# Attention over a cached K and V with a squared-ReLU gate: PV turned to queries on partitions, and FFN, projections and out-projection as fillers

## The chip, the core and the metric

The kernel runs on one core of one Trainium2 chip. The metric is device time in microseconds (us) of one execution, the median of three runs. Before the change it is 1469.16 us (1469.04 to 1469.86).

The engines are named as the profile names them: PE multiplies matrices (PEld is its weight load), DVE and ACT work on vectors, POOL on small things, and SP issues DMAs. SBUF holds tiles of 128 partitions, PSUM holds the results of PE in banks of 512 f32 columns per partition.

## The reference

x has 2048 rows of 512. There are 32 heads of width 128, each with 2048 cached keys and values. All inputs are bf16.

```
xn = (x - mean) / sqrt(var + 1e-5)
q  = xn @ wq                        # 32 heads of 128
p  = softmax(q @ k_cache^T * 128**-0.5)
s  = (p @ v_cache) @ wo             # [2048, 512]
h  = relu(xn @ w1 + b1) ** 2        # [2048, 1792]
g  = silu(h @ w2 + b2)
out = x + s * g
```

## The kernel before, in words

Queries are cut into 4 blocks of 512 (index j), keys into 16 tiles of 128, taken in 8 pairs. One pair of key tiles of one head of one block is a step (index `pi`, 4 x 32 x 8 = 1024 of them); a head of a block has the index `g` (128 of them), the step within it is `k`.

The program is written as one list of instructions per engine, in the order in which the Python code emits them; each engine runs its list strictly in that order, and waits on semaphores where an operand or a buffer needs it. So the place of a call in the code decides what queues behind what.

It has two stages. The first one, which the code calls phase A, loads the whole of x transposed (`xnT`, features on partitions), does the layernorm in that form with ones-matmuls for the sums, and then the FFN of all four blocks (`gen_ffn`: 14 chunks of 128 hidden features, `gen_hT`, `gen_relu_sq`, `gen_o2`), up to the gate `g_all` of all 2048 queries. Its SBUF is then given free, and everything of the second stage that may reuse it waits for the end of phase A.

The second stage runs the 1024 steps (L805). A step emits two score matmuls into `psA` (`gen_scores`, keys on partitions, 512 queries on columns, two buffers of 1024 columns), an exp on ACT into `pT` (`gen_exp`), additions of `pT` into `accD` on DVE for the denominators (`gen_den_adds`), extras, and the PV of two steps earlier (`gen_pv`). PV has V as weights and 512 columns of `pT` moving; its result in `psB` has head features on partitions and queries on columns.

Since the queries lie on columns, a denominator per query has to be spread over all 128 partitions. `gen_headend_A` (in step k = 2 of the next head) sums `accD` over partitions by four 1-column matmuls, takes the reciprocal, and writes it onto the diagonals of `diag_t`; `gen_headend_B` (k = 4) multiplies ones by `diag_t` into `psC`, copies it to `rrep`, and multiplies `psB` by it into `oT_all`. The other extras are the projection of the head after next (`gen_proj`, 4 matmuls into `psC` and a copy to `qt_sb`) and, from block 1 on, one out-projection matmul of the block before in four of the eight steps (`gen_post_tasks`, 32 heads accumulated in `psD` for one tile of 128 queries, then times `g_all` plus x). The last block's out-projection stands behind the loop.

K is loaded by a transposing DMA on SP's queue two heads ahead into three buffers, V and `wq` by plain ones.

All matmuls go through one helper (L149), so the profile tells them apart by their tiles.

Of the kernel before, what the change touches and what calls it, by code (L numbers as in the profile page):

```python
# [43 lines left out]
class _Sched:  # L44
# [42 lines left out]
    def emit(self, eng, fn, deps=()):  # L87
        waits = self._resolve(eng, deps)
        idx = eng.n
        eng.n += 1  # L90
        eng.prog.append((waits, fn, ("cnt",)))
        return _Tok(eng.sem, idx + 1, dict(eng.known))
# [58 lines left out]

def _act(e, out, in_, func, scale=1.0, bias=0.0):
    return e.activation(out, in_, func, bias=bias, scale=scale)  # L153
# [28 lines left out]
def _iota(e, out):  # L182
    return e.iota(out, [[1, out.shape[-1]]], base=0, channel_multiplier=-1,
                  allow_small_or_imprecise_dtypes=True)
# [15 lines left out]
def bass_recurrent_scan__mha_block_cached__dense_activation_squared_relu__prompt_kernel(  # L200
# [12 lines left out]
    dbg_xnT=None,  # L213
    dbg_g=None,
    dbg_s=None,
    stage="full",
# [4 lines left out]
    assert Dh == P and D % P == 0 and D <= 512 and F % P == 0  # L221
    assert Sq % 512 == 0 and Sk % (2 * P) == 0
    QB = 512
    NQT = Sq // P
# [9 lines left out]
    NPAIR = NG * NPR  # L234

# [8 lines left out]
    ones = nc.alloc_sbuf_tensor("ones", [P, P], BF16)  # L244
    ident = nc.alloc_sbuf_tensor("ident", [P, P], BF16)
    xnT = nc.alloc_sbuf_tensor("xnT", [P, NDC, Sq], BF16)
    g_all = nc.alloc_sbuf_tensor("g_all", [P, NQT, D], BF16)

    psA = nc.alloc_psum_tensor("psA", [P, 4 * 512], F32)
    psB = nc.alloc_psum_tensor("psB", [P, 2 * 512], F32)  # L250
    psC = nc.alloc_psum_tensor("psC", [P, 512], F32)
    psD = nc.alloc_psum_tensor("psD", [P, 512], F32)

    def bankA(i):
        return psA[:, i * 512:(i + 1) * 512]

    def bankB(i):
        return psB[:, i * 512:(i + 1) * 512]

    sl_out = [S.slot("out0"), S.slot("out1")]  # L260
    sl_dbg = S.slot("dbg")

    from contextlib import ExitStack
    stackA = ExitStack()
    sbA = lambda shape, dt, name: stackA.enter_context(nc.sbuf_tensor(name, shape, dt))
    xT_sq = sbA([P, NQB, NDC, QB], BF16, "xT_sq")
    var_t = sbA([P, NQB, QB], F32, "var_t")
    lnv_t = sbA([P, NQB, QB], F32, "lnv_t")
    rstd_t = sbA([P, NQB, QB], BF16, "rstd_t")
    w1_sb = sbA([P, NDC, F], BF16, "w1_sb")  # L270
    w2_sb = sbA([P, NFC, D], BF16, "w2_sb")
    r_t = sbA([P, 2, QB], BF16, "r_t")
    NH2 = 3
    h2T = sbA([P, NH2, QB], BF16, "h2T")
    sig_t = sbA([P, 2, D], BF16, "sig_t")
    identf = sbA([P, P], F32, "identf")
    b1b = sbA([P, NFC], BF16, "b1b")
    b1f = sbA([P, NFC], F32, "b1f")
    b2row = sbA([P, D], BF16, "b2row")
    _phaseA_hwm = nc.sbuf_base  # L280

    t_ones = E(GP, partial(_memset, out=ones[:], val=1.0))
    t_idf = E(GP, partial(_iota, out=identf[:]))
    t_ident = E(GP, partial(_ts, out=ident[:], in0=identf[:], scalar1=0.0, scalar2=None,
                           op0=ALU.is_equal), deps=[t_idf])

    sl_x = [S.slot(f"xT{c}") for c in range(NDC)]
    sl_w = S.slot("wmisc")

    tok_xc = [None] * NDC  # L290
    for c in range(NDC):
        tok_xc[c] = S.emit_dma(
            SP, partial(_dmaT, out=xnT[:, c, :], in_=A_x[0, :, c * P:(c + 1) * P]),
            sl_x[c])
    tok_x = tok_xc[-1]
    S.emit_dma(SP, partial(_dma, out=w1_sb[:], in_=B_w1.rearrange("(c p) f -> p c f", p=P)),
               sl_w, group_done=False)
    S.emit_dma(SP, partial(_dma, out=w2_sb[:], in_=B_w2.rearrange("(c p) d -> p c d", p=P)),
               sl_w, group_done=False)
    S.emit_dma(SP, partial(_dma_gather, nc, out=b1b[:], in_=B_b1.rearrange("(c p) -> p c", p=P)),  # L300
               sl_w, group_done=False)
    tok_w = S.emit_dma(SP, partial(_dma, out=b2row[0:1, :],
                                   in_=B_b2.rearrange("(o d) -> o d", o=1)),
                       sl_w, group_done=True)
    t_b1 = E(DV, partial(_copy, out=b1f[:], in_=b1b[:]), deps=[tok_w])

    invD = 1.0 / float(D)
    assert NQB <= 4, "LN schedule assumes <= 4 query blocks (psA banks)"
    t_scale_last = [None] * NQB
    t_psA_reader = [None] * 4  # L310
    t_sums = [None] * NQB
    for j in range(NQB):
        js = slice(j * QB, (j + 1) * QB)
        for c in range(NDC):
            t_sums[j] = E(PE, partial(_mm, out=bankA(j)[:, :], lhsT=ones[:, :], rhs=xnT[:, c, js],
                                      start=(c == 0), stop=(c == NDC - 1)),
                          deps=[t_ones, tok_xc[c]])
    t_ctr_all, t_sq_all = [], []
    for j in range(NQB):
        js = slice(j * QB, (j + 1) * QB)  # L320
        t_ctr = []
        for c in range(NDC):
            t_ctr.append(E(DV, partial(_stt, out=xnT[:, c, js], in0=bankA(j)[:, :], scalar=-invD,
                                       in1=xnT[:, c, js], op0=ALU.mult, op1=ALU.add),
                           deps=[t_sums[j]]))
        t_psA_reader[j] = t_ctr[-1]
        t_ctr_all.append(t_ctr)
        t_sq = []
        for c in range(NDC):
            t_sq.append(E(AC, partial(_act, out=xT_sq[:, j, c, :], in_=xnT[:, c, js],  # L330
                                      func=ACT.Square),
                          deps=[t_ctr[c]]))
        t_sq_all.append(t_sq)
    t_ss_reader = [None, None]
    t_v = [None] * NQB
    for j0 in range(0, NQB, 2):
        grp = list(range(j0, min(j0 + 2, NQB)))
        t_ss = {}
        for j in grp:
            s = j % 2  # L340
            psS = psC if s == 0 else psD
            for c in range(NDC):
                t_ss[j] = E(PE, partial(_mm, out=psS[:, :], lhsT=ones[:, :], rhs=xT_sq[:, j, c, :],
                                       start=(c == 0), stop=(c == NDC - 1)),
                            deps=[t_sq_all[j][c], t_ss_reader[s], t_ones])
        for j in grp:
            s = j % 2
            psS = psC if s == 0 else psD
            t_v[j] = E(DV, partial(_ts, out=var_t[:, j, :], in0=psS[:, :], scalar1=invD,
                                   scalar2=LN_EPS, op0=ALU.mult, op1=ALU.add),  # L350
                       deps=[t_ss[j]])
            t_ss_reader[s] = t_v[j]
    t_l = [None] * NQB
    for j in range(NQB):
        t_l[j] = E(AC, partial(_act, out=lnv_t[:, j, :], in_=var_t[:, j, :], func=ACT.Ln),
                   deps=[t_v[j]])
    t_r = [None] * NQB
    for j in range(NQB):
        t_r[j] = E(AC, partial(_act, out=rstd_t[:, j, :], in_=lnv_t[:, j, :], func=ACT.Exp,
                               scale=-0.5),  # L360
                   deps=[t_l[j]])
    for j in range(NQB):
        js = slice(j * QB, (j + 1) * QB)
        t_sc = None
        for c in range(NDC):
            t_sc = E(DV, partial(_tt, out=xnT[:, c, js], in0=xnT[:, c, js],
                                 in1=rstd_t[:, j, :], op=ALU.mult),
                     deps=[t_r[j], t_sq_all[j][c]])
        t_scale_last[j] = t_sc

    t_g_done = [None] * NQT
    t_gtile_reader = [None] * TPB
    t_psB_reader = [None, None]
    t_r_reader = [None, None]
    t_h2_reader = [None] * NH2
    t_sig_reader = [None, None]
    ffn_state = {"chunk_ctr": 0}

    def gen_ffn(j):
        js = slice(j * QB, (j + 1) * QB)  # L380

        def gen_bias():
            for qt in range(TPB):
                E(PE, partial(_mm, out=bankA(qt)[:, 0:D], lhsT=ones[0:1, 0:P], rhs=b2row[0:1, 0:D],
                              start=True, stop=False),
                  deps=[tok_w, t_ones, t_gtile_reader[qt], t_psA_reader[qt]])

        def gen_hT(c, slot_b):
            t = None
            for dc in range(NDC):  # L390
                t = E(PE, partial(_mm, out=bankB(slot_b)[:, :],
                                  lhsT=w1_sb[:, dc, c * P:(c + 1) * P], rhs=xnT[:, dc, js],
                                  start=(dc == 0), stop=(dc == NDC - 1)),
# [28 lines left out]
        for c in range(NFC):  # L422
# [3 lines left out]
            if c == min(1, NFC - 1):  # L426
                gen_bias()
# [438 lines left out]
```

## Time and profile before

| what | value |
|---|---|
| median of 3 runs | 1469.16 us (1469.04 to 1469.86) |
| profiled execution, span | 1469.5 us |
| PE / DVE / ACT busy | 1305.6 / 1171.9 / 1055.7 us |
| phase A (layernorm, FFN) | from 0 to about 163 us |
| attention steps | from about 163 to 1429 us |
| out-projection of the last block, output | from about 1429 us on |
| mean granted TensorE clock | 0.983 |

The page gives each engine's busy time with its share of the span, the chain of work that ended last, and groups of instructions (line, engine, operation, tile written <- tiles read, shape, count, busy us, mean ns of one, idle time just before and what ended it). A row of a stretch (windows) has the engines' busy times in turn, with counts in brackets, the granted clock, the share in which the 16 DMA engines were busy, and GB/s. A timeline row has start, length, engine, instruction. Matmuls overlap in a stream, so the mean time of one is longer than the distance from one start to the next.

### The profile page before, as it was taken

To read this page: it belongs to the slowest core of one execution; us is meant where nothing else is said; L and a number is where in the kernel's file an instruction comes from. 1 tells how busy PE (TensorE), PEld (TensorE's weight loads), DVE (VectorE), ACT (ScalarE), POOL (GpSimd) and SP (SyncE) were. 2 spreads that over 40 slices of the span, in tenths; PEclk is the share of its full clock that TensorE was granted. 3 is DMA by queue.
4 is the path that set the end of the run, shared out by engine and by line. 5 is a ranking of instruction groups with operands and counts; after the bars stand their busy time and mean duration, and the time that the engine had idled before them with its cause. 6 is when DMAs were issued, how large, how long until landed. Compare 5 with 4: busy or idle time off the path is not lost.

```text
span 1469.5 us, 17842 instructions
## 1 busy us (share of the span) xinstructions
PE 1305.6 (89%) x6640; PEld 572.3 (39%) x6640; DVE 1171.9 (80%) x2117; ACT 1055.7 (72%) x1069; POOL 19.7 (1%) x43
## 2 busy tenths in 40 slices
PE   3899888888888999999999999999999999999987
PEld 0334333333333444444444444444444444444433
DVE  2666688888888888888888888888888888888871
ACT  2210588887778888888888888888888888888860
POOL 0000000000000000000000000000000000000001
PEclk7899999999999999999999999999999999999999
DMA  9100267777666656655755665655655665666510
GB/s 227 31 0 0 41 128 158 157 151 149 119 124 129 124 110 128 128 119 115 136 112 122 129 121 113 136 114 116 134 118 120 125 130 110 130 125 121 113 36 25
DMA packets 616265, 166.33 MB, mean 113 GB/s; under 512 B 608754, under 2 KB 614643, under 8 KB 616179
## 3 DMA queue, kind: packets, MB, share of 16 engines
q1 hardware_dynamic: 614642, 160.99, 55.3%
q0 software_dynamic: 1536, 4.20, 0.8%
q8 instruction: 53, 0.87, 0.3%
q14 instruction: 34, 0.27, 0.1%
HBM read 93.85 MB, written 2.10 MB: 65 GB/s over the span
## 4 chain that ended last, share of the span: by engine, by line
PE 60%; DVE 23%; ACT 13%; issue 2%; SPq 1%; DMA 1%; DVEq 0%; POOL 0%
PE psA L149 22%; PE psB L149 22%; ACT pT L153 12%; PE psC L149 11%; DVE accD L157 10%; DVE diag_t L157 6%; PE psD L149 6%; DVE rden_b L171 2%; DVE rden_t L175 1%; DVE tmp_t L157 1%; SPq L192 1%; ACT xT_sq L153 1%; DVE out_t L157 1%; DVE g_all L157 1%; DMA b2row<-in_B_b_dram 1%
## 5 line engine op out<-in xcount | busy, mean ns | idle before, releaser
L153 ACT ACTIVATE pT<-psA 128x1024 bf16<-128x1024 f32 x1024 | 1026.0, 1024 | 237.2 <-PE psA L149 214.6
L157 DVE TENSOR_TENSOR accD<-accD,pT 128x1024 bf16<-128x1024 bf16 x896 | 617.9, 690 | 173.9 <-ACT pT L153 149.2
L149 PE MATMUL psA<-qt_sb,kT 128*128 128x512 bf16 x2048 | 610.2, 380 | 0.3 <-ACT pT L153 0.3
L149 PE MATMUL psB<-pT,v_sb 128*128 128x512 bf16 x2048 | 609.0, 379 | 0.3 <-ACT pT L153 0.3
L149 PEld LDWEIGHTS psA<-qt_sb,kT 128*128 128x128 bf16 x2048 | 196.8, 98 | 247.2 <-ACT pT L153 26.2
L149 PEld LDWEIGHTS psB<-pT,v_sb 128*128 128x128 bf16 x2048 | 185.4, 98 | 182.8 <-ACT pT L153 1.1
L149 PE MATMUL psD<-wo_all,oT_all 128*128 128x512 bf16 x512 | 176.4, 385 | 2.4 <-DVE tmp_t L157 2.4
L149 PE MATMUL psC<-xnT,wq_sb 128*128 128x512 bf16 x512 | 152.7, 381 | 3.4 <-DVE qt_sb L171 3.2
L149 PE MATMUL psC<-diag_t,ones 128*128 128x128 bf16 x512 | 51.0, 222 | 113.0 <-DVE diag_t L157 113.0
L149 PEld LDWEIGHTS psC<-diag_t,ones 128*128 128x128 bf16 x512 | 29.0, 98 | 175.5 <-DVE diag_t L157 175.5
L157 DVE TENSOR_TENSOR diag_t<-ident,rden_b 128x512 bf16<-128x512 bf16 x128 | 88.6, 692 | 4.4
L157 DVE TENSOR_TENSOR oT_all<-psB,rrep 128x512 bf16<-128x512 f32 x128 | 88.5, 691 | 4.4
L171 DVE CAST qt_sb<-psC 128x512 bf16<-128x512 f32 x128 | 87.5, 683 | 2.0 <-PE psC L149 2.0
L171 DVE CAST rrep<-psC 128x512 bf16<-128x512 f32 x128 | 87.5, 684 | 0.7 <-PE psC L149 0.7
L153 ACT ACTIVATE sig_t<-psA 128x512 bf16<-128x512 f32 x16 | 9.1, 596 | 105.4 <-PE psA L149 104.3
L149 PEld LDWEIGHTS psD<-wo_all,oT_all 128*128 128x128 bf16 x512 | 50.4, 99 | 65.3 <-DVE tmp_t L157 3.8
L149 PEld LDWEIGHTS psC<-xnT,wq_sb 128*128 128x128 bf16 x512 | 47.7, 97 | 71.0 <-issue 38.3
L163 DVE TENSOR_SCALAR r_t<-psB,b1f 128x512 bf16<-128x512 f32 x56 | 42.0, 750 | 27.9 <-PE psB L149 27.9
L149 PE MATMUL psB<-xnT,w_sb 128*128 128x512 bf16 x224 | 59.4, 392 | 4.9 <-DVE xnT L157 4.9
L149 PE MATMUL psA<-w_sb,h2T 128*128 128x512 bf16 x224 | 58.5, 384 | 4.5 <-DVE h2T L157 4.5
L157 DVE TENSOR_TENSOR accD<-accD 128x512 bf16<-128x512 bf16 x128 | 54.4, 425 | 4.4
L171 DVE COPY accD<-pT 128x1024 bf16<-128x1024 bf16 x128 | 53.3, 417 | 1.2 <-ACT pT L153 1.2
(37 smaller groups left out, 289.0 us busy)
## 6 DMA issues: line engine op xcount, KB each, us to landing
v_sb<-in_A_v_cache_dram SPq DMA_DIRECT2D x128, 512.0 KB, 4.7
wq_sb<-in_A_wq_dram SPq DMA_DIRECT2D x128, 128.0 KB, 4.7
wo_all<-in_A_wo_dram SPq DMA_DIRECT2D x4, 1024.0 KB, 6.1
w_sb<-in_B_w_dram SPq DMA_DIRECT2D x2, 1792.0 KB
kT<-in_A_k_cache_dram SPq DMA_TRANSPOSE x128, 4.6
x_t<-in_A_x_dram POOLq DMA_DIRECT2D x16, 128.0 KB, 3.9
out_dram<-out_t POOLq DMA_DIRECT2D x16, 128.0 KB, 3.7
xnT<-in_A_x_dram SPq DMA_TRANSPOSE x4, 5.1
```

The costliest lines, as they stand in the source:

```text
L149: return e.matmul(out, lhsT, rhs, start=start, stop=stop)
L153: return e.activation(out, in_, func, bias=bias, scale=scale)
L157: return e.tensor_tensor(out, in0, in1, op)
L163: return e.tensor_scalar(out, in0, scalar1=scalar1, scalar2=scalar2, op0=op0, op1=op1)
L171: return e.tensor_copy(out, in_)
L175: return e.reciprocal(out, in_)
L192: return e.dma_start(out, in_, transpose=True)
```

## The change

The second kernel computes the same. Nearly every function is written anew:

- **PV** has a 128 x 128 piece of `pT` as weights and V as the moving operand, with a column of ones behind V's 128 columns (`VW`, buffers set to one at the start). A step has 8 matmuls of 129 columns in the place of 2 of 512. The result `psO` has queries on partitions, and its 129th column is the denominator. The `accD` additions, the 1-column matmuls, `diag_t`, `rrep` go. At the end of a head DVE copies `psO` to `o_un` (two copies, one a bank), takes the reciprocal and multiplies into `o_bf`; a transposing DMA from SBUF to SBUF brings it into `oT` with features on partitions. `psO` has two banks for the four query tiles, and no second set.
- **Layernorm** works with queries on partitions (bn_stats, bn_aggr, a power on POOL), a block at a time; a transposing DMA writes `xnT`. Block 0 is done ahead of the loop, the others in it.
- **FFN, projections and out-projection** are jobs in a sorted list, each with a step from which it may run and one by which it is wanted. A job is a run of matmuls into one of two banks of `psF` and an evacuation on DVE. `fill_one` emits one matmul of the current job; a step gets up to two, by a credit that spreads them evenly, between its scores and the PV of two steps earlier. The out-projection goes by chunks of 8 heads, summed in `acc`.
- **silu** is z (1 + tanh(z / 2)) / 2; the half is put into the combination.
- `emit(..., inc=False)` leaves out a semaphore increment for matmuls that nobody waits for.

Core of the diff:

```diff
-            t = EB(PE, partial(_mm, out=bankB(b)[:, :], lhsT=v_sb[:, sidx, tt, :],
-                               rhs=pT[:, g % 2, k, i * QB:(i + 1) * QB],
-                               start=(tt == 0), stop=(tt == NKT - 1)),
-                   deps=[t_exp[pi], t_vfill[g], t_norm[g - 2] if g >= 2 else None])
+        order = [(n, qt) for n in range(2) for qt in range(TPB)]
+        if last:
+            order = [(n, qt) for b in range(2) for qt in (2 * b, 2 * b + 1) for n in range(2)]
...
+            t = E(PE, partial(_mm_shared, out=psO[:, b, qt % 2, 0:Dh + 1],
+                              lhsT=pT[:, pi % NPT, n * QB + qt * P:n * QB + (qt + 1) * P],
+                              rhs=v_sb[:, i, tt, 0:Dh + 1],
+                              start=(tt_first and qt % 2 == 0), stop=(tt == NKT - 1)),
+                  deps=[t_exp[pi], t_vfill[g], t_ones,
+                        t_oev[g - 1][b] if g >= 1 else None], inc=inc)
...
+            for b in range(2):
+                t_oev[g][b] = E(DV, partial(_copy, out=o_un[:, s, 2 * b:2 * b + 2, 0:Dh + 1],
+                                            in_=psO[:, b, :, 0:Dh + 1]),
+                                deps=[t_bank[b], t_onorm[g - 2] if g >= 2 else None])
+            tr = E(DV, partial(_recip, out=rden[:, s, :], in_=o_un[:, s, :, Dh]),
+                   deps=[t_oev[g][0], t_oev[g][1], t_onorm[g - 2] if g >= 2 else None])
...
+            t_onorm[g] = E(DV, partial(_tt, out=o_bf[:, s, :, :], in0=o_un[:, s, :, 0:Dh], in1=rb,
+                                       op=ALU.mult),
+                           deps=[tr, tok_oT[g - 2] if g >= 2 else None])
...
+    def gen_oT(g):
+        chunk = g // HC
+        tok_oT[g] = S.emit_dma(
+            SP, partial(_dmaT, out=oT[:, g % NOT, :].rearrange("p (t q) -> p t q", q=P),
+                        in_=o_bf[:, g % 2, :, :].rearrange("p t d -> p (t d)")), sl_oT[g % 4],
+            deps=[t_onorm[g], t_wodone.get(chunk - NOT // HC)])
...
+    for g in range(2, NG):
+        jobs.append((NPR * (g - 2) - 2, NPR * (g - 2), job_proj(g)))
+    for j in range(NQB):
+        b = j * (SPB - NPR)
+        for c in range(NFC):
+            k = b + 6 + (SPB * 8 // 256) * c
+            jobs.append((k, k - 40, job_h(j, c)))
+        for qt in range(TPB):
+            k = b + SPB // 2 - 4 + (SPB * 28 // 256) * qt
+            jobs.append((k, k - 40, job_o2(j, qt)))
+        b = j * SPB
+        for m in range(NCH):
+            for qt in range(TPB):
+                r = b + HC * NPR * (m + 1) + 14
+                jobs.append((r + 2 + 12 * qt, r, job_wo(j, m, qt)))
+    jobs.sort(key=lambda x: x[0])
...
+    for pi in range(NPAIR):
+        g, k = divmod(pi, NPR)
+        gen_scores(pi)
+        credit = min(credit + left[0] / (NPAIR - pi), 8.0)
+        n = 0
+        while n < 3:
+            late = bool(jobs) and jobs[0][0] + 8 <= pi
+            if not (credit >= 1.0 or late) or n == 2 or not fill_one(pi):
+                break
+            credit = max(credit - 1.0, 0.0)
+            left[0] -= 1
+            n += 1
...
+        if pi >= LAG:
+            gen_pv(pi - LAG)
+        if k == 0:
+            fill_wq(g + 3)
+            fill_k(g + 2)
+        if k == LAG - 1:
+            fill_v(g + 2)
+        if k == LAG + 1 and g >= 1:
+            gen_oT(g - 1)
```

How it stands on PE, around the middle of the program. Before, in block 1 (`psD` is the out-projection, the 128x1 and 128x128 rows are the denominators of the head before):

```order
L149 MATMUL psA<-qt_sb,kT 128x512 x2
L149 MATMUL psC<-ones,accD 128x1 x4
L149 MATMUL psB<-pT,v_sb 128x512 x2
L149 MATMUL psA<-qt_sb,kT 128x512 x2
L149 MATMUL psD<-wo_all,oT_all 128x512
L149 MATMUL psB<-pT,v_sb 128x512 x2
L149 MATMUL psA<-qt_sb,kT 128x512 x2
L149 MATMUL psC<-diag_t,ones 128x128 x4
```

The changed kernel, steps k = 1 and 2 of a head (`psF` are the fillers; the first `psO` row ends the head before, the second begins the new one and needs `psO` copied out):

```order
L152 MATMUL psA<-qt_sb,kT 128x512 x2
L152 MATMUL psF<-wo_all,oT 128x512
L157 MATMUL psO<-v_sb,pT 128x129 x8
L152 MATMUL psA<-qt_sb,kT 128x512 x2
L152 MATMUL psF<-wo_all,oT 128x512
L152 MATMUL psF<-xnT,wq_sb 128x512
L157 MATMUL psO<-v_sb,pT 128x129 x8
```

The denominator rows are gone; each step now holds scores, one or two fillers and eight short matmuls.

On DVE, one head in the same part of the program, before:

```order
L171 COPY accD<-pT 128x1024
L157 TENSOR_TENSOR accD<-accD,pT 128x1024 x2
L175 RECIPROCAL rden_t<-psC 128x4
L171 CAST rden_b<-rden_t 128x4
L157 TENSOR_TENSOR diag_t<-ident,rden_b 128x512
L157 TENSOR_TENSOR accD<-accD,pT 128x1024 x2
L171 CAST rrep<-psC 128x512
L157 TENSOR_TENSOR oT_all<-psB,rrep 128x512
L157 TENSOR_TENSOR accD<-accD,pT 128x1024 x3
L157 TENSOR_TENSOR accD<-accD 128x512
L171 CAST qt_sb<-psC 128x512
```

and in the changed kernel, a head with the evacuation of a second FFN matrix tile (`z_t`) among its rows:

```order
L179 COPY o_un<-psO 128x2x129 x2
L183 RECIPROCAL rden<-o_un 128x4
L165 TENSOR_TENSOR o_bf<-o_un,rden 128x512
L165 TENSOR_TENSOR z_t<-psF,b2bc 128x512
L179 CAST qt_sb<-psF 128x512
L175 SCALAR_TENSOR_TENSOR g_all<-th_t,z_t 128x512
```

The additions over `pT` are gone; what stands in their place are two copies out of `psO`, one product, and the fillers' evacuations wherever a job ends.

At the start, PE had the FFN of a block as one run of its own:

```order
L149 MATMUL psB<-xnT,w_sb 128x512 x8
L149 MATMUL psA<-b2row,ones 128x512 x4
L149 MATMUL psA<-w_sb,h2T 128x512 x4
L149 MATMUL psB<-xnT,w_sb 128x512 x4
L149 MATMUL psA<-w_sb,h2T 128x512 x4
```

In the changed kernel the first rows are already a projection and the scores of the first steps, and the FFN's matmuls with `w_sb` stand between them:

```order
L152 MATMUL psF<-xnT,wq_sb 128x512 x8
L152 MATMUL psA<-qt_sb,kT 128x512 x2
L152 MATMUL psF<-xnT,wq_sb 128x512
L152 MATMUL psA<-qt_sb,kT 128x512 x2
L152 MATMUL psF<-xnT,wq_sb 128x512
L152 MATMUL psA<-qt_sb,kT 128x512 x2
L152 MATMUL psF<-xnT,wq_sb 128x512 x2
L157 MATMUL psO<-v_sb,pT 128x129 x8
L152 MATMUL psA<-qt_sb,kT 128x512 x2
L152 MATMUL psF<-xnT,w_sb 128x512
```

So the run of FFN matmuls ahead of the attention is gone from PE's list, and stands in pieces of one or two within its steps.

More of the change, by code (lines that the diff above doesn't have):

```diff
@@ L271, in bass_recurrent_scan__mha_block_cached__dense_activation_squared_relu__prompt_kernel @@
[L271 to L285, printed above, removed]
@@ L310, in bass_recurrent_scan__mha_block_cached__dense_activation_squared_relu__prompt_kernel @@
[L310 to L333, printed above, removed]
@@ new lines, in evac, with job_h, mm @@
+        def evac(bank, step):
+            t_evac[g] = E(DV, partial(_copy, out=qt_sb[:, g % NQS, :], in_=bankF(bank)),
+                          deps=[t_proj[g], t_S_last[g - NQS] if g >= NQS else None])
+            return t_evac[g]
+        return NDC, mm, evac
+    def job_h(j, c):
+        js = slice(j * QB, (j + 1) * QB)
+        box = [None]
+        def mm(n, bank):
+            box[0] = E(PE, partial(_mm, out=bankF(bank), lhsT=w1_sb[:, n, c * P:(c + 1) * P],
+                                   rhs=xnT[:, n, js], start=(n == 0), stop=(n == NDC - 1)),
+                       deps=[tok_w1, t_bankF[bank]] + tok_xT[j], inc=(n == NDC - 1))
+        def evac(bank, step):
+            s = c % 2
+            t1 = E(DV, partial(_ts, out=r_t[:, s, :], in0=bankF(bank), scalar1=b1f[:, c:c + 1],
+                               scalar2=0.0, op0=ALU.add, op1=ALU.max),
+                   deps=[box[0], t_b1, t_rt[s]])
+            t_h2[j, c] = t_rt[s] = E(
+                DV, partial(_tt, out=h2T[:, c, :], in0=r_t[:, s, :], in1=r_t[:, s, :],
+                            op=ALU.mult),
+                deps=[t1] + [t_o2.get((j - 1, qt)) for qt in range(TPB)])
+            return t1
+        return NDC, mm, evac
@@ new lines, in job_o2, with mm, evac, tanh @@
+    def job_o2(j, qt):
+        jt = j * TPB + qt
+        def mm(n, bank):
+            t = E(PE, partial(_mm, out=bankF(bank), lhsT=h2T[:, n, qt * P:(qt + 1) * P],
+                              rhs=w2_sb[:, n, :], start=(n == 0), stop=(n == NFC - 1)),
+                  deps=[tok_w2, t_bankF[bank], t_h2[j, n]], inc=(n == NFC - 1))
+            if t is not None:
+                t_o2[j, qt] = t
+        def evac(bank, step):
+            s = jt % 2
+            tz = E(DV, partial(_tt, out=z_t[:, s, :], in0=bankF(bank), in1=b2bc[:], op=ALU.add),
+                   deps=[t_o2[j, qt], tok_b2, t_zrd[s]])
+            box = [None]
+            def tanh():
+                box[0] = E(AC, partial(_act, out=th_t[:, s, :], in_=z_t[:, s, :], func=ACT.Tanh,
+                                       scale=0.5), deps=[tz, t_thr[s]])
+            def gate():
+                gs = jt % (2 * TPB)
+                t_g[jt] = t_zrd[s] = t_thr[s] = E(
+                    DV, partial(_stt, out=g_all[:, gs, :], in0=th_t[:, s, :], scalar=1.0,
+                                in1=z_t[:, s, :], op0=ALU.add, op1=ALU.mult),
+                    deps=[box[0], t_fin.get(jt - 2 * TPB)])
+            at(step + 1, tanh)
+            at(step + 3, gate)
+            return tz
+        return NFC, mm, evac
@@ L835, in bass_recurrent_scan__mha_block_cached__dense_activation_squared_relu__prompt_kernel @@
+    assert not jobs and cur[0] is None and not events
+    fin = [_Tok(sl.sem, sl.val) for sl in sl_out + sl_fin]
     S.emit_wait(GP, fin)
```

790 lines of the change are left out of this document (305 added, 485 removed).

## The prediction

> **What bounds the kernel now.** I read the page first (busy shares, chain, costliest groups), then the waits, then the engines by stage.
>
> ```profile
> span 1469.5 us, 17842 instructions
> PE 1305.6 (89%) x6640; PEld 572.3 (39%) x6640; DVE 1171.9 (80%) x2117; ACT 1055.7 (72%) x1069; POOL 19.7 (1%) x43
> PE 60%; DVE 23%; ACT 13%; issue 2%; SPq 1%; DMA 1%; DVEq 0%; POOL 0%
> L153 ACT ACTIVATE pT<-psA 128x1024 bf16<-128x1024 f32 x1024 | 1026.0, 1024 | 237.2 <-PE psA L149 214.6
> L157 DVE TENSOR_TENSOR accD<-accD,pT 128x1024 bf16<-128x1024 bf16 x896 | 617.9, 690 | 173.9 <-ACT pT L153 149.2
> PE psC L149 <- DVE diag_t L157: 113.0, 128, 1.2
> core 0: us, PE busy (x) PEld busy (x) DVE busy (x) ACT busy (x) POOL busy (x), PEclk, DMA share, GB/s
> 0.00:45.00 45.00, 15.50 (x32) 3.96 (x32) 13.68 (x26) 17.88 (x27) 2.17 (x11) 0.74 0.95 210
> 45.00:163.00 118.00, 108.41 (x470) 45.84 (x471) 80.12 (x142) 11.85 (x19) 0.75 (x1) 0.96 0.01 2
> 170.00:465.00 295.00, 261.39 (x1363) 108.57 (x1362) 255.40 (x464) 237.73 (x249) 0.00 (x0) 1.00 0.70 139
> 783.00:1101.00 318.00, 291.86 (x1532) 132.09 (x1533) 268.38 (x485) 259.29 (x255) 4.33 (x8) 1.00 0.61 122
> 1425.00:1469.50 44.50, 32.23 (x139) 13.50 (x138) 10.35 (x17) 0.39 (x1) 4.88 (x9) 0.88 0.09 27
> ```
>
> No engine fills the span, for two reasons. The stages stand one behind the other: 163 us of layernorm and FFN hold almost no exp, and 44 us at the end hold only the last block's out-projection. And in the attention stage PE, DVE and ACT each stand at 80 to 92% and lock step: 128 times, once a head, PE waits some 0.9 us for `diag_t`, the last link of the denominator chain on DVE, and ACT then starves.
>
> **What one matmul costs.** The change turns PV round, so the price of a 129-column matmul with a fresh weight load decides. Three stretches of the timeline (start, us, what) give prices; the last two rows are one 32-matmul stretch of the tail and the group that it belongs to.
>
> ```profile
> 800.73 0.24 PE L149 MATMUL psC<-ones,accD 128*128 128x1 bf16 x4
> 800.84 0.59 PE L149 MATMUL psB<-pT,v_sb 128*128 128x512 bf16 x2
> 803.76 0.40 PE L149 MATMUL psC<-diag_t,ones 128*128 128x128 bf16 x4 [0.82 <-DVE diag_t L157]
> 803.99 0.59 PE L149 MATMUL psB<-pT,v_sb 128*128 128x512 bf16 x2
> 1439.85 7.08 PE L149 MATMUL psD<-wo_all,oT_all 128*128 128x512 bf16 x32 [0.79 <-DVE tmp_t L157]
> L149 PE MATMUL psD<-wo_all,oT_all 128*128 128x512 bf16 x512 | 176.4, 385 | 2.4 <-DVE tmp_t L157 2.4
> ```
>
> A 512-column matmul in a stream takes (7.08 - 0.385) / 31 = 0.216 us, its weight load hidden. Four 128-column matmuls, each with its own load, take 803.99 - 803.76 = 0.23 us, 57.5 ns each. Four 1-column ones take 0.11 us: 27.5 ns for a load and next to no streaming. So a load passes in at most 27.5 ns, and 128 columns cover it. One more column is (216 - 57.5) / 384 = 0.4 ns: **57.9 ns** for the new form. Its bounds are 54.4 ns (0.216 x 129 / 512) and 27.5 + 54.4 = 81.9 ns (no overlap); I stay by the 57.5 ns row, the nearest in form, though bursts of four are all that it shows.
>
> The Trainium skill, page "TensorE: Matmul & The Clock Gate", section "Back-to-back issue gap", speaks against the change here: it gives about 81 ns per matmul at 128 columns for a sustained stream of load and matmul pairs, against 56 ns alone. The diag row agrees with the smaller figure; the same sentence's 131 ns for 512 columns is contradicted by the 216 ns above. By its 81 ns the sum below would end at about 1480 us.
>
> **The steady loop.** There are 1024 steps (32 heads x 4 query blocks x 8 pairs of key tiles). Each has 2 score matmuls, 8 PV matmuls and 0 to 2 fillers; counted in the program, 1432 fillers lie in the loop (504 projection, 224 + 224 FFN, 480 out-projection). PE: 2048 x 0.216 = 442.4, PV 8192 x 0.0579 = 474.3 (2048 x 0.216 = 442.4 before), fillers 1432 x 0.216 = 309.3, sum **1226.0 us**, 1.2 us a step. The `accD` sums, denominator and `diag_t` matmuls, the bias matmuls and the layernorm sums on PE all go.
>
> ```profile
> 808.73 4.14 ACT L153 ACTIVATE pT<-psA 128x1024 bf16<-128x1024 f32 x4 [0.27 <-PE psA L149]
> L153 ACT ACTIVATE sig_t<-psA 128x512 bf16<-128x512 f32 x16 | 9.1, 596 | 105.4 <-PE psA L149 104.3
> ```
>
> ACT needs (4.14 - 1.024) / 3 = 1.04 us a step, below PE. Only 18 steps without a filler (PE 0.895) are set by ACT: 18 x 0.144 = 2.6 us. The 16 tanh, about 0.6 us like `sig_t`, fall into ACT's spare 0.16 us a step and the two score buffers; uncovered they would cost 10 us. The program holds one table load, so no switching. Loop: **1228.6 us**.
>
> **The new wait.** `psO` exists once. The first PV of a head waits until DVE has copied the last head's sums out of it, and the next scores, hence exps, are queued behind that PV.
>
> ```profile
> 1446.97 0.69 DVE L157 TENSOR_TENSOR tmp_t<-psD,g_all 128x512 f32<-128x512 f32 x1 [6.45 <-PE psD L149]
> 1447.72 7.08 PE L149 MATMUL psD<-wo_all,oT_all 128*128 128x512 bf16 x32 [0.79 <-DVE tmp_t L157]
> L171 DVE CAST qt_sb<-psC 128x512 bf16<-128x512 f32 x128 | 87.5, 683 | 2.0 <-PE psC L149 2.0
> L175 DVE RECIPROCAL rden_t<-psC 128x4 f32<-128x4 f32 x128 | 22.4, 175 | 0.4 <-PE psC L149 0.4
> L157 DVE TENSOR_TENSOR oT_all<-psB,rrep 128x512 bf16<-128x512 f32 x128 | 88.5, 691 | 4.4
> L163 DVE TENSOR_SCALAR r_t<-psB,b1f 128x512 bf16<-128x512 f32 x56 | 42.0, 750 | 27.9 <-PE psB L149 27.9
> L157 DVE TENSOR_TENSOR h2T<-r_t 128x512 bf16<-128x512 bf16 x56 | 23.8, 425 | 1.9
> ```
>
> From PE's last streamed column (1439.85 + 32 x 0.216 = 1446.76) to DVE's start is 0.21 us; from DVE's end (1447.66) to PE 0.06. A copy of 2 x 129 columns lies between the 4-column 175 ns and the 512-column 683 ns; in proportion 0.43 us. Let bank 0's last column stream at 0; bank 1 follows at 0.23. The copies end at 0.64 and 1.07, PE sees 1.13. PE reaches bank 1's first matmul of the next head at 0.23 + 0.43 + 0.12 and the fillers: 1.0 with one, 1.21 with two. So a head with one filler waits 0.14 us, with two nothing. If a filler group ended just ahead of that PV, its evacuation stands first on DVE: 0.68 more for a projection, 1.18 (r_t, then h2T) for an FFN chunk, 0.69 for the out-projection. Counted in the program's order over 127 head changes: 93 have none (53 of them with one filler, 53 x 0.14 = 7.4), 14 a projection (8.6), 12 an FFN chunk (11.9), 8 another (4.3). Sum **32 us**; bounds 0, if DVE were always in time, and 127 x 1.0 = 127, if it were always as late as behind an FFN chunk. DVE itself is no bound: (0.86 + 0.18 + 0.69 + 0.68) x 128 = 308 and some 185 for the rest (56 x 1.18, 144 x 0.69, layernorm), under 40% of the span.
>
> **Head.** Layernorm now takes one block of 512 queries, on DVE and by transposing DMAs, and stands alone before the first scores.
>
> ```profile
> 0.73 10.01 SPq L192 DMA_TRANSPOSE xnT<-in_A_x_dram  x4
> 13.23 5.34 PE L149 MATMUL psA<-xnT,ones 128*128 128x512 bf16 x13 [1.68 <-DMA xnT<-in_A_x_dram]
> v_sb<-in_A_v_cache_dram SPq DMA_DIRECT2D x128, 512.0 KB, 4.7
> kT<-in_A_k_cache_dram SPq DMA_TRANSPOSE x128, 4.6
> xnT<-in_A_x_dram SPq DMA_TRANSPOSE x4, 5.1
> out_dram<-out_t POOLq DMA_DIRECT2D x16, 128.0 KB, 3.7
> L162 POOL TENSOR_SCALAR ident<-identf 128x128 bf16<-128x128 f32 x1 | 0.5, 541 | 0.1
> L157 DVE TENSOR_TENSOR xnT<-xnT,rstd_t 128x512 bf16<-128x512 bf16 x16 | 5.5, 417 | 2.6 <-ACT rstd_t L153 2.6
> ```
>
> The 512 KB of x land at 0.73 + 4.7 = 5.4. The trace shows no bn_stats; four passes over 512 columns cost 0.42 to 0.75 each, with four 0.18 aggregates 2.4 to 3.7, say 3.3 with the small add; the power on POOL about 0.5. Four scalings end at about 11; the transposes take 0.6 (a quarter of 10.01 / 4) to 2.5 us to issue and 5.1 to land: 16.6, at worst 25. Four matmuls at the cold 5.34 / 13 = 0.41 us and the evacuation bring the first scores to **19 us**. Behind them SP queues V, K, wq, then `w1` and `w2`. The FFN's first filler, in step 3, needs `w1`: some 4.1 MB from 10 us on at 210 GB/s, so at 30 us where PE comes at 23. `wq` of head 3 follows `w2` and is some 3 us late. Stalls **10 us** (0 to 20).
>
> **Tail.** After the last scores: exp and last PV 1; copies, reciprocal, normalising 2; the transposing DMA of `oT` 0.6 + 4.6; of the last 32 out-projection matmuls 7 run meanwhile, 25 are left, 8 of them cold, 7.1; combination 1.6; output 0.5 + 3.7. Together **21 us** (15 to 27).
>
> Sum: 1228.6 + 32 + 29 + 21 = **1311 us** against a profiled 1469.5, which stands 0.02% above the median 1469.16, so nothing is corrected.
>
> **Other queues.** DMA was busy 0.70 x 295 = 206 us over 249 / 8 = 31 heads, 6.6 us a head. `oT` adds 128 KB to 1152: 0.7 us by bytes. If a transpose out of SBUF took as long as a whole `kT` (512 of 1152 KB, 2.9 us), it would be 9.5 of the 9.9 us that a head now takes: still covered, with nothing to spare. On SP, `oT` waits for DVE's normalising in a head's step 3, behind that head's loads, which run two heads ahead; the out-projection that needs it is released 11 steps later.
>
> **Rivals.** (a) *Loads are not hidden in a long stream.* The place is PV. At 81.9 ns PV costs 670.9 us, the loop 1422.6; heads wait less, 15 us; 1422.6 + 15 + 29 + 21 = **1488, slower**. It decides from (1469 - 65 - 751.7) / 8192 = 79.6 ns. For it: 64 such matmuls a head where the trace has only fours. Against it: the 57.5 ns. 11%. The Trainium skill's 81 ns, named above, would be this case. (b) *The wait for `diag_t` returns as a wait for `psO`.* At 1.0 us each head: 1279 + 127 = **1406**. Against it: DVE falls from 80% to 40%. 7%. (c) *DMA becomes the bound*: `oT` dear and the queue at 9.5 us a head, PE waits some 0.4 us a head, 50 us: **1361**. 7%. (d) *The FFN does not hide*: the loop's count of 1432 fillers excludes it.
>
> **The numbers.** Forecast 75%, 1262 to 1385 by itself. Lower ends together (54.4 ns, no head waits, shorter ends) give 1237; these are not likely at once. Range 1260 to 1400: it takes in (c), most of (b), and leaves out (a). About 0.2% is what a measurement can tell from no change. Faster 0.87, same 0.02, slower 0.11.
>
> **What would show it.** PV's 129-column group at 58 ns from start to start; PE above 93% busy, first named in the chain; some 1.0 to 1.1 us ACT period with no engine wait but `psO` on DVE `o_un`, about 30 us; DVE near 40%; first scores at 19 us; PE's wait for `w_sb` under 20 us. It is wrong if PV's pitch is near 80 ns, if PE waits for ACT in every step, or if loads land late.

## The result, and the profile after

The changed kernel takes 1287.39 us (median of 4, 1287.09 to 1290.29), the kernel before 1469.51 in the same call: a ratio of 0.876, 95% interval 0.875 to 0.878. The prediction was 1311 (1260 to 1400). The profiled execution took 1287.63 us, 1.8 us of them outside its span.

From the page of the changed kernel, in this order: span, busy line, chain, four groups; then two rows of its waits, and one stretch of its windows (PE, PEld, DVE, ACT and POOL busy, clock, DMA share, GB/s):

```profile
span 1285.8 us, 26303 instructions
PE 1231.2 (96%) x11506; PEld 807.6 (63%) x11712; DVE 472.0 (37%) x949; ACT 1052.9 (82%) x1041; POOL 21.6 (2%) x42
PE 93%; DVE 3%; issue 1%; DMA 1%; SPq 1%; POOL 0%
L161 ACT ACTIVATE pT<-psA 128x1024 bf16<-128x1024 f32 x1024 | 1044.9, 1023 | 214.1 <-PE psA L152 170.4
L157 PE MATMUL psO<-v_sb,pT 128*128 128x129 bf16 x8192 | 638.9, 220 | 13.2 <-DVE o_un L179 11.9
L179 DVE COPY o_un<-psO 128x258 f32<-128x258 f32 x256 | 97.0, 421 | 229.6 <-PE psO L157 228.5
L165 DVE TENSOR_TENSOR o_bf<-o_un,rden 128x512 bf16<-128x512 f32 x128 | 88.6, 692 | 4.6 <-DVE rden L183 0.3
PE psO L157 <- DVE o_un L179: 11.9, 16, 2.5
PE psF L152 <- DMA wq_sb<-in_A_wq_dram: 5.1, 1, 5.1
400.00:700.00 300.00, 292.99 (x2757) 192.75 (x2806) 110.54 (x224) 252.80 (x250) 4.30 (x7) 1.00 0.79 141
```

PE has taken over the chain: 93% where it had 60%. DVE, second before with 80% busy and 23% of the chain, is at 37% and 3%. In the steady stretch PE is at 98% and ACT at 84%. Most of ACT's idle time is put down to PE (the row of `pT`), and the list of waits has no row of PE for ACT. The DMA queue rose from 55.3 to 76.7% of the engines' time, and between the first 31 us and the tail no wait of PE is put down to it.

The price of the new PV can be read from two steps of the timeline (start, us, what; 604.06 is the first score matmul of a step):

```profile
604.06 0.59 PE L152 MATMUL psA<-qt_sb,kT 128*128 128x512 bf16 x2
604.49 0.59 PE L152 MATMUL psF<-xnT,wq_sb 128*128 128x512 bf16 x2
604.92 0.62 PE L157 MATMUL psO<-v_sb,pT 128*128 128x129 bf16 x8
605.38 0.59 PE L152 MATMUL psA<-qt_sb,kT 128*128 128x512 bf16 x2
605.81 0.38 PE L152 MATMUL psF<-xnT,wq_sb 128*128 128x512 bf16 x1
606.02 0.62 PE L157 MATMUL psO<-v_sb,pT 128*128 128x129 bf16 x8
606.48 0.59 PE L152 MATMUL psA<-qt_sb,kT 128*128 128x512 bf16 x2
```

In 2.42 us lie 7 matmuls of 512 columns (1.51 us at 0.216) and 16 of 129: 0.91 / 16 = **56.7 ns**. Over the whole loop, the mean distance from one PV matmul's start to the next, leaving out those lengthened by a wait, is the same 56.7 ns.

### The profile page after: what moved, and what is told of

Its sections match the earlier page's. It is cut to its first block, busy times and chain, and to the rows that moved or that the text cites. A ratio compares the mean times of both kernels' runs of the same rounds, so it can differ in the third digit from the quotient of the medians.

```text
span 1285.8 us, 26303 instructions
## 1 busy us (share of the span) xinstructions
PE 1231.2 (96%) x11506; PEld 807.6 (63%) x11712; DVE 472.0 (37%) x949; ACT 1052.9 (82%) x1041; POOL 21.6 (2%) x42
## 3 DMA queue, kind: packets, MB, share of 16 engines
q1 hardware_dynamic: 685536, 180.41, 76.7%
q8 instruction: 92, 1.51, 0.5%
## 4 chain that ended last, share of the span: by engine, by line
PE 93%; DVE 3%; issue 1%; DMA 1%; SPq 1%; POOL 0%
PE psO L157 36%; PE psA L152 33%; PE psF L152 24%; DVE r_t L171 1%; SPq L203 1%; DVE st_t L191 1%; DVE o_un L179 0%; DVE h2T L165 0%; DMA wq_sb<-in_A_wq_dram 0%; DMA x_ln<-in_A_x_dram 0%; DMA oT<-o_bf 0%; DVE mv_t L195 0%; DVE qt_sb L179 0%; DVE xn_t L171 0%; DVE acc L175 0%
## 5 line engine op out<-in xcount | busy, mean ns | idle before, releaser
L157 PEld LDWEIGHTS psO<-v_sb,pT 128*128 128x128 bf16 x8192 | 546.4, 98 | 268.8 <-issue 39.4
L157 PE MATMUL psO<-v_sb,pT 128*128 128x129 bf16 x8192 | 638.9, 220 | 13.2 <-DVE o_un L179 11.9
L152 PE MATMUL psF<-xnT,wq_sb 128*128 128x512 bf16 x510 | 177.0, 385 | 22.2 <-DMA xnT<-xn_t 17.1
L179 DVE COPY o_un<-psO 128x258 f32<-128x258 f32 x256 | 97.0, 421 | 229.6 <-PE psO L157 228.5
L152 PE MATMUL psF<-wo_all,oT 128*128 128x512 bf16 x510 | 170.2, 383 | 2.6 <-DMA oT<-o_bf 2.5
L179 DVE CAST qt_sb<-psF 128x512 bf16<-128x512 f32 x128 | 88.4, 691 | 190.9 <-PE psF L152 190.8
L152 PEld LDWEIGHTS psF<-xnT,wq_sb 128*128 128x128 bf16 x512 | 50.5, 99 | 84.1 <-issue 19.5
L165 DVE TENSOR_TENSOR o_bf<-o_un,rden 128x512 bf16<-128x512 f32 x128 | 88.6, 692 | 4.6 <-DVE rden L183 0.3
L152 PE MATMUL psF<-xnT,w_sb 128*128 128x512 bf16 x224 | 76.1, 379 | 0.1
L152 PE MATMUL psF<-w_sb,h2T 128*128 128x512 bf16 x221 | 73.0, 379 | 0.0
```

The lines of the kernel that those rows point to most:

```text
L152: return e.matmul(out, lhsT, rhs, start=start, stop=stop)
L157: return e.matmul(out, lhsT, rhs, start=start, stop=stop, skip_group_check=True)
L165: return e.tensor_tensor(out, in0, in1, op)
L179: return e.tensor_copy(out, in_)
```

## The experiments

Theory: the loop is the sum of PE's matmuls, and what stands above it are waits for DVE at head changes, set by DVE's order. The rivals: the gaps are ACT's; the gain is the turned PV alone, or the interleaving alone; weight loads take longer than 27.5 ns.

### The base again

The changed kernel was run once more, with no edit, as the base of the next three, which ran in the same call.

> The changed kernel once more, as the base of this call. Both theories: 1287 us, 0.876 of before, with some 23 us of waits of PE for the copies of psO at the 127 head changes, two of them (at 100 and 410 us) over 2 us long.

Measured: 1290.62 us, 0.8778 (0.8766 to 0.8790). The kernel moves by 3 us from call to call, so smaller steps are read only within one call. The later experiments ran in other calls, and their differences from 1287 us carry those 3 us.

### Evacuations behind PV, statistics later

What stands ahead of the copies of `psO` at a head change? Two places of the changed kernel's timeline:

```profile
940.65 0.75 DVE L171 TENSOR_SCALAR r_t<-psF,b1f 128x512 bf16<-128x512 f32 x1 [2.83 <-PE psF L152]
941.33 0.38 PE L152 MATMUL psF<-xnT,wq_sb 128*128 128x512 bf16 x1
941.44 0.43 DVE L165 TENSOR_TENSOR h2T<-r_t 128x512 bf16<-128x512 bf16 x1
941.78 0.75 DVE L179 COPY o_un<-psO 128x258 f32<-128x258 f32 x2
942.34 0.76 PE L157 MATMUL psO<-v_sb,pT 128*128 128x129 bf16 x8 [0.63 <-DVE o_un L179]
...
406.21 0.69 DVE L191 BATCH_NORM_STATS2 st_t<-x_ln 128x6 f32<-128x512 bf16 x1
409.53 0.17 DVE L170 TENSOR_SCALAR ve_t<-mv_t 128x4 f32<-128x4 f32 x1
409.61 0.76 DVE L179 COPY o_un<-psO 128x258 f32<-128x258 f32 x2
410.17 0.76 PE L157 MATMUL psO<-v_sb,pT 128*128 128x129 bf16 x8 [2.50 <-DVE o_un L179]
```

At 942 an FFN chunk's evacuation runs first; at 410 the next block's layernorm statistics hold DVE for 3.4 us. The first edit defers the evacuations of a step until its PV stands in DVE's list, the second moves the statistics by four steps:

```diff
         if i == n - 1:
-            t_bankF[bank] = evac(bank, step)
+            late_evac.append((bank, evac, step))
...
         if pi >= LAG:
             gen_pv(pi - LAG)
+        flush()
```

```diff
-            at(j * SPB + 7 * NPR, partial(ln_stats, j + 1))
+            at(j * SPB + 7 * NPR + 4, partial(ln_stats, j + 1))
```

> A filler's evacuation on DVE is put behind the PV of the same step, so at a head change the copies of psO stand ahead of it. Theory (the waits come from what stands ahead of the copies in DVE's order): the waits of 0.3 to 0.8 us at some 30 head changes go, 10 to 14 us in all, 1275 us; the two long ones stay. Rival one (the copy's own 0.76 us and two latencies are the wait): no change, 1287. Rival two (a later evacuation frees the filler bank later and PE waits there instead): 1287 or more, with PE waiting for DVE at psF.

> The layernorm statistics of the next block (4 x 0.67 and 4 x 0.18 us on DVE) are put four steps later, away from the head change. Theory: the two or three waits of 2.2 to 2.5 us go, 5 to 7 us in all, 1281 us. Rival (those long waits come from x arriving late, not from DVE's order): they move along, no change.

Measured: 1272.50 us, 0.8658 (0.8646 to 0.8670), 18 less than the base, more than the 10 to 14 expected; and 1282.52, 0.8727 (0.8715 to 0.8739), 8 less. The first has these rows among its waits, the second this one:

```profile
PE psO L157 <- DVE o_un L179: 4.1, 2, 2.5
...
PE psO L157 <- DVE o_un L179: 7.5, 15, 0.7
```

Without the evacuations ahead, two waits are left of 16, one of them the long one of 2.5 us; without the statistics ahead, 15 are left and the longest is 0.7. These rows count idle time from the modelled end of the last matmul, so they show less than the delay. Taken from the starts of PE's matmuls in the traces, the first PV of a head is late by 24 us in all in the changed kernel, by 8 with the evacuations behind PV and by 19 with the statistics later. Both rivals of the first fail: the copies by themselves cost little, and no wait of `psF` for a later evacuation appeared in the loop.

### All moves together, and the start

> Evacuations behind PV, statistics four steps later, two fillers forced into the step ahead of a head's first PV, and the third wq load put ahead of V and the second K at the start. Theory (loop = sum of PE's matmuls at 216 and 56.7 ns, 1218 us, plus the waits): nearly all 23 us of waits go and 5 us at the start, 1260 us. Rival (the gaps are ACT's, which then takes over as the bound at uneven steps): no less than 1275.

The edit adds to the two above:

```diff
-            if not (credit >= 1.0 or late) or n == 2 or not fill_one(pi):
+            want = n < 2 if (k == LAG and g >= 1) else credit >= 1.0 or late
+            if not want or n == 2 or not fill_one(pi):
...
     fill_wq(1)
+    fill_wq(2)
     ln_stats(0)
```

Measured: 1267.18 us, 0.8622 (0.8610 to 0.8634), 23 under the base, not 30. The waits at head changes are nearly gone (by the starts, 1.5 us are left of 24), but the start gained nothing: the 5.1 us for `wq_sb` came back as 6.0 for `w_sb`. So `w1` was put ahead of the second K and V as well, and a fourth kernel did the same without the forced fillers:

> The kernel with all four moves, and w1 loaded ahead of the second K and V. Theory (PE's wait at the start is the order of SP's queue): the 6 us wait for w_sb goes, 1261 us. Rival (the bytes ahead of the first 30 us have to land anyway, and the wait moves to kT or v_sb): 1267.

> As the one before, without the two fillers forced into the step ahead of a head's first PV. Theory (with DVE's order right, the copies' own 0.76 us make PE wait some 0.1 us at a head change with one filler): 5 to 10 us more than with them. Rival (the copies are in time by themselves): the same within 2 us.

Measured: 1267.18, 0.8624 (0.8612 to 0.8636), and 1269.19, 0.8633 (0.8619 to 0.8648). The wait rows of PE for loads, of the kernel with all moves first, then with `w1` ahead:

```profile
PE psF L152 <- DMA w_sb<-in_B_w_dram: 6.0, 1, 6.0
...
PE psF L152 <- DMA wq_sb<-in_A_wq_dram: 4.2, 1, 4.2
PE psF L152 <- DMA w_sb<-in_B_w_dram: 1.1, 1, 1.1
```

Both rivals had the time right. The first named the wrong load, though: the wait did not move to `kT` or `v_sb`. Of the 6.0 us for `w1`, 1.1 are left, and 4.2 now stand 11 us later, for the `wq` of the fourth head, which is queued behind `w2`. With the first stall gone PE comes to it sooner, so 5.3 us of 6.0 remain. And the forced fillers are worth no more than 2 us, inside the intervals: a head change with one filler needs little help. All three kernels, at 1267 to 1269 us, are faster than both kernels of this case.

### PV back to V as weights

Two kernels keep all of the changed kernel but the form of PV; one without denominators, one with the additions on DVE again:

```diff
-            t = E(PE, partial(_mm_shared, out=psO[:, b, qt % 2, 0:Dh + 1],
-                              lhsT=pT[:, pi % NPT, n * QB + qt * P:n * QB + (qt + 1) * P],
-                              rhs=v_sb[:, i, tt, 0:Dh + 1],
+            t = E(PE, partial(_mm, out=psO[:, g % 2, :], lhsT=v_sb[:, i, tt, 0:Dh],
+                              rhs=pT[:, pi % NPT, n * QB:(n + 1) * QB],
```

> PV alone put back to V as weights and 512 columns of pT moving, into two psO banks taken in turn; fillers and all else stay. Denominators and normalising are left out and the output's layout is wrong. Theory (PE is the bound and PV costs the same either way): PV 2048 x 0.216 = 442 for 8192 x 0.0567 = 464, and no wait at head changes: 1287 - 22 - 23 = 1242 us. Rival (the gain of the change lies in the turned PV's matmuls themselves): slower than 1287.

> As the one before, with the additions of pT into accD on DVE put back (7 x 0.69 + 0.42 us a head, 671 us in all), whose sum is not used; denominators are left out. DVE is then busy about 472 - 120 + 671 = 1020 us. Theory (turning PV pays by freeing DVE, which would else be late for the fillers' evacuations): some waits of PE for DVE, 1250 to 1300 us. Rival one (DVE becomes the bound through its order): over 1350. Rival two (DVE's load never mattered): 1242 as without.

Measured: 1239.41 us (0.842, 0.839 to 0.845) and 1257.31 (0.854, 0.852 to 0.857). Both fall where the theory put them. The turned PV does not pay on PE: its matmuls and the head changes cost 1287 - 1239 = 48 us more than the old form without denominators. And 671 us of additions, which bring DVE to 78% busy, cost only 18 us in the same call. That leaves the rest of the denominator chain, so a third kernel put all of it back (1-column matmuls and `diag_t` in the filler's other bank, `rrep`, product into `oT`):

```diff
+        if k == LAG + 1 and g >= 1:
+            headend_A(g - 1)
+        if k == LAG + 3 and g >= 1:
+            headend_B(g - 1)
         if pi >= LAG:
             gen_pv(pi - LAG)
...
-        if k == LAG + 1 and g >= 1:
-            gen_oT(g - 1)
```

> The changed kernel with its PV turned back whole: V as weights, accD additions, 1-column matmuls, diag_t, rrep and the product into oT as before, each in its place in a head, the fillers as they are. By sum: PE 1218 - 464 + 442 + 128 x 0.34 = 1239 us, no wait for psO copies; DVE 983 + 128 x (0.43 + 0.18 + 0.17 + 0.69 + 0.68) = 1258 us, so both engines need about the span. Theory (the turned PV pays through DVE, which is freed from 97% busy to 37%): DVE's order makes PE wait, 1320 to 1400 us. Rival (the gain of the change is the interleaving alone, the turned PV adds nothing): 1285 to 1300 us.

Measured: 1411.00 us, 0.9597 (0.9583 to 0.9611). Its busy line, chain, and three rows of its waits:

```profile
PE 1278.2 (91%) x6463; PEld 577.0 (41%) x6592; DVE 1233.3 (88%) x2229; ACT 1046.5 (74%) x1041; POOL 24.8 (2%) x48
PE 58%; DVE 37%; issue 3%; DMA 1%; SPq 1%; ACT 0%; DVEq 0%; POOL 0%; ACTq 0%
PE psF L152 <- DVE qt_sb L179: 47.3, 56, 4.4
ACT pT L161 <- DVE accD L165: 58.2, 108, 3.4
DVE rden_t L183 <- PE psF L152: 37.5, 82, 1.3
```

PE and DVE wait for each other in turn: DVE for the sums from PE, PE for a filler bank behind DVE's additions, ACT for a `pT` buffer that an addition still reads. Neither engine is full, and the sum of PE, some 1240 us, is far off. The time lies 11 us above the range of the theory, and over 100 above the rival's. By this undo, of the 182 us that the change gains, everything but the turned PV (the interleaving, with the new layernorm and out-projection) gives 1469.7 - 1411.0 = 59, and turning PV the other 124 (to 1287). The undo puts the denominators into a bank that the fillers use too, in steps 3 and 5 of a head. Another placement of them was not run, so the 124 us hold for this one.

### The kernel before with its wait moved

```diff
-        if k == clamp(4) and g >= 1:
+        if k == clamp(5) and g >= 1:
             items.append(lambda: gen_headend_B(g - 1))
...
-            if k == clamp(6):
-                items.append(lambda: gen_proj(g + 2, 0))
-            if k == NPR - 1:
-                items.append(lambda: gen_proj(g + 2, 1))
+            if k == NPR - 1:
+                items.append(lambda: gen_proj(g + 2))
```

> The kernel before, with the broadcast of the denominators one step later in the head and the projection in one piece at the head's end. Theory (in before the loop lost its time to the wait for diag_t, not to the adds): the 113 us of waits go, bounded by ACT's 8.3 and PE's 9.0 us a head: 1469 - 100 = 1370, with the first 163 and last 40 us as they are. Rival (the additions on DVE are the bound of a head, 80% busy): less than 30 us gained.

Measured: 1457.73 us, 0.9905 (0.9874 to 0.9937): 14 us less, where the theory had 100. Its chain, what is left of the old wait, and the wait that came in its place:

```profile
DVE 43%; PE 37%; ACT 13%; issue 4%; SPq 1%; DMA 1%; DVEq 0%; POOL 0%
PE psC L149 <- DVE diag_t L157: 8.3, 32, 1.2
PE psC L149 <- DVE rrep L171: 76.0, 125, 1.1
```

The theory was wrong here, and the rival had the time right: the wait for `diag_t` was where the order of DVE showed, not the cause. Moved by a step, it came back one link on, and the chain went over to DVE. This agrees with the full undo above. That the additions alone are the bound, as the rival put it, is not shown: beside the fillers, without the rest of the chain, they cost 18 us.

### Work left out

> The changed kernel with the FFN's matmuls, evacuations and tanh left out (the gate is a constant). Theory (PE is the bound in every step, so a filler costs its matmul's time): 448 x 0.216 = 97 us less, 1190 us, and ACT at 1045 of it. Rival (fillers fall into time that PE would spend waiting for ACT): 1250 or more.

The FFN's jobs were struck from the list and `g_all` set to ones. Measured: 1185.50 us, 0.8056 (0.8031 to 0.8080): 102 us less than 1287, for 97 of matmuls, so the rival's 1250 is refuted. A filler costs its matmul, and nothing in the loop hides it.

> Only 65 of the 129 columns of V are multiplied (half of the head's features are left out, the ones column stays). Theory (weight loads pass in 27.5 ns and hide under the columns): 30 ns a matmul, a step's eight in 0.24 us, PE's loop 1000 us, so ACT becomes the bound at 1.04 us a step: about 1115 us. Rival (a load takes some 55 ns by itself and the columns hid under it): 55 ns a matmul as now, 1285 us.

```diff
-                              rhs=v_sb[:, i, tt, 0:Dh + 1],
+                              rhs=v_sb[:, i, tt, 64:Dh + 1],
```

Measured, one run: 1088.62 us. From its timeline, and its chain:

```profile
600.95 0.41 PE L157 MATMUL psO<-v_sb,pT 128*128 128x65 bf16 x8
601.17 0.13 PEld L152 LDWEIGHTS psA<-qt_sb,kT 128*128 128x128 bf16 x2
601.20 0.59 PE L152 MATMUL psA<-qt_sb,kT 128*128 128x512 bf16 x2
...
1046.81 22.11 ACT L161 ACTIVATE pT<-psA 128x1024 bf16<-128x1024 f32 x24
PE 82%; DVE 5%; ACT 5%; DMA 3%; issue 2%; SPq 1%; POOL 0%
```

Eight matmuls of 65 columns, each with its own load, take 601.20 - 600.95 = 0.25 us, 31 ns each, as against 30 expected. So a load passes in 31 ns or less, and the loads are not what sets 56.7 ns at 129 columns: the rival is refuted. The other half of the theory failed: ACT did not become the bound. The chain has PE at 82% and ACT at 5%, and 24 exps (of 1.027 us each by their own record) follow each other at (22.11 - 1.027) / 23 = 0.92 us, not at the 1.04 taken from the kernel before. PE's sum at 31 ns is 1006 us; how the rest of the 1088 divides between start, tail and waits was not worked out.

## Why the prediction was right, and where its terms were off

The steps held: the steady loop is PE's sum, the loads hide, DVE and DMA are no bounds, the new wait is the one for `psO`. Against the span of 1285.8 us the sum of 1311 was 25 too long (the last PV stands in two of the measured rows, so these add up to 1 us more than the span):

| term | predicted, us | measured, us |
|---|---|---|
| PV, 8192 matmuls | 474.3 (57.9 ns) | 464.5 (56.7 ns) |
| other matmuls of the loop, ACT's 18 steps | 754.3 | 751 (no sign of ACT's) |
| waits at head changes | 32 | 24 |
| first scores | 19 | 20.3 |
| stalls at the start | 10 | 7.6 |
| tail | 21 | 19.3 |

**PV.** 10 of the 25 us. The four diag matmuls from which 57.5 ns were read follow a wait, and at hundredths of a us such a short stretch gives no more. The Trainium skill ("TensorE: Matmul & The Clock Gate", "Back-to-back issue gap") gives N / 2.4 + 2.5 ns for a matmul by itself, from which 56.2 at 129 columns is an estimate; the trace agrees with that, and its 8192 matmuls contradict the 81 ns that the same section gives at 128 columns for a sustained stream.

**ACT's steps.** 2.6 of the 25 us. Steps without a filler were put down to ACT at 1.04 us. In the trace the PV of three such steps starts at 101.17, 102.05 and 102.94, 0.885 us apart, which is PE's own sum, so ACT did not set them; its exps can follow each other in 0.92 us, as the run with 65 columns shows.

**Waits at head changes.** Some 8 us. The rule was right (what stands ahead of the copies decides), the sizes were not. Heads with one filler and no evacuation ahead were given 0.14 us each, 7.4 in all. By the starts in the trace they are late by 0.03 each, which agrees with the 2 us or less that the forced fillers recover: the two copies take 0.75 us together, where 0.86 was summed. An FFN chunk ahead was given 1.0 us with one filler; the row at 942.34 stands 0.79 after PE could have begun (941.33 + 0.216). Taking the evacuations away gained 15 (to the first 1287) to 18 us, for 25 predicted. And one item was not in the sum: the statistics of the next block, 2.2 to 2.5 us at a head change, worth 5 to 8 us by their experiment.

**Start.** Its size was nearly right, its culprit was not, so the size is in part luck. The stalls forecast were for `w1` and, 3 us, for the `wq` of the fourth head; the trace has 5.1 us for the `wq` of the third head, queued on SP behind V, the second K and the second V:

```profile
17.06 3.44 PE L152 MATMUL psF<-xnT,wq_sb 128*128 128x512 bf16 x8 [17.06 <-DMA xnT<-xn_t]
20.34 0.59 PE L152 MATMUL psA<-qt_sb,kT 128*128 128x512 bf16 x2
26.05 0.61 PE L152 MATMUL psF<-xnT,wq_sb 128*128 128x512 bf16 x1 [5.11 <-DMA wq_sb<-in_A_wq_dram]
30.98 0.39 PE L152 MATMUL psF<-xnT,w_sb 128*128 128x512 bf16 x1
```

From 20.34 to 30.98 PE had 12 matmuls of 512 columns and 8 of PV to do, 3.05 us: 7.6 lost. Some 5.3 of them are the wait (20.77 to 26.05), the other 2.3 slower matmuls behind it (last section). The first matmul on `w1` then started at 30.98, where 30 had been forecast, so the first wait only took the place of the second; the two reordered starts show the same from the other side, and there the `wq` of the fourth head does come late, by 4.2 us. The first scores came 1.3 us late: eight matmuls of two projections stand ahead of them, where four were summed.

**The rivals.** Loads not hidden (1488): refuted, in the trace and by 65 columns. The wait for `psO` at every head (1406): refuted, 16 waits are named in 127 heads, and by the starts they are late by 24 us, not 127. DMA as the bound (1361): the queue took 0.79 x 300 / (250 / 8) = 7.6 us a head, between the 7.3 by bytes and the 9.5 of the rival, and nothing in the loop waited for it.

What the prediction did not say is how the gain divides: the full undo of the turned PV, as it was placed, shows about a third for the rest of the change and two thirds for the turned PV, the latter not by what it does on PE (there the old form is 48 us cheaper) but by ending the exchange between PE and DVE within each head.

## What to carry to other kernels

A wait that the profile names between two engines may be only where a loop over both shows: moving it gained 14 us of 113, taking the exchange itself away 124 in another form of the kernel. Once one engine's sum is the time, every filler costs its own price, and the rest is to be had from what stands ahead of a release in another engine's list: deferring evacuations behind it was worth 18 us for a few lines. Reordering loads at the start of this kernel twice moved the wait to another load and gained nothing.

## What the runs showed of the hardware that was not expected

A wait of PE can cost more than its length. Behind the 5.1 us at the start, six matmuls of 512 columns took from 26.05 to 28.58, 0.42 us each where 0.216 is usual (the first is quoted above; the changed kernel's timeline goes on, and the last row is a stretch of it):

```profile
26.45 1.06 PE L152 MATMUL psA<-qt_sb,kT 128*128 128x512 bf16 x2
27.30 0.63 PE L152 MATMUL psF<-xnT,wq_sb 128*128 128x512 bf16 x1
27.73 1.06 PE L152 MATMUL psA<-qt_sb,kT 128*128 128x512 bf16 x2
28.58 0.63 PE L152 MATMUL psF<-xnT,wq_sb 128*128 128x512 bf16 x1
...
26.00:30.00 4.00, 3.96 (x14) 1.76 (x15) 0.32 (x1) 2.05 (x2) 0.00 (x0) 0.50 1.02 399
```

Shorter waits differ. Four windows, columns as in the stretch above: of the changed kernel behind the 2.50 us for `psO` that end at 410.17; of its second run, where the same wait of 2.50 us ends at 409.43; of the kernel with evacuations behind PV, where a wait of 2.50 us at the same place ends at 405.16; and of the changed kernel's tail, behind 2.50 us for `oT` that end at 1272.42.

```profile
410.00:413.00 3.00, 2.83 (x31) 2.01 (x32) 1.83 (x5) 1.52 (x2) 3.00 (x5) 1.00 0.46 95
```

```profile
410.00:413.00 3.00, 3.00 (x19) 1.88 (x18) 1.16 (x2) 1.02 (x1) 2.26 (x5) 0.61 0.48 121
```

```profile
407.00:410.00 3.00, 3.00 (x18) 1.84 (x16) 0.00 (x0) 1.44 (x2) 0.99 (x2) 0.53 0.90 211
```

```profile
1272.00:1275.00 3.00, 2.58 (x8) 0.98 (x9) 2.66 (x5) 0.00 (x0) 0.00 (x0) 0.65 0.00 0
```

The granted clock was 0.50 behind the 5.1 us. Behind the waits of 2.50 us it stayed at 1.00 in the first window and fell to 0.61, 0.53 and 0.65 in the other three. The Trainium skill ("TensorE: Matmul & The Clock Gate", "HAM oscillation — how this bites in real kernels") puts the point from which it falls at some 3.4 us of idleness; the 5.1 us agree, the 2.50 us do not, and here the measurement decides: a wait of 2.5 us can be enough. The place in the program does not decide it, since the first two windows are one wait of one kernel in two executions; what does no run settled.

Exps of 128 x 1024 followed each other in 0.92 us in the run with 65 columns, less than the 1.027 us that each takes by its own record.

The power on POOL took 1.04 us for 128 x 4 elements; I had estimated 0.5 from a 128 x 128 operation of 0.54 us.
